# Squares by products, table rows for the sampled blocks, casts with two possible engines, and weights spread wider in a block-sparse attention and feed-forward kernel

## The chip, the cores and the metric

The kernel runs on one core of a Trainium2 chip. The time is what one execution takes on the device, in microseconds (us); several executions give a median. A profile shows one further execution, instruction by instruction. The engines are named as the profile names them: PE (matrix products), PEld (its weight loads), DVE (vector engine), ACT (scalar engine), POOL (GpSimd) and SP, whose queue starts nearly all transfers.

## The reference, cut to what matters

Four batches, eight heads, 768 positions of 64 numbers each. A query block of 32 positions sees its neighbours, the first and last block and three sampled blocks; the first and last query blocks see everything. The attention output is the input of a feed-forward layer with a maximum over three products.

```python
scores = scale * np.matmul(q, k.transpose(0, 1, 3, 2))
mask = np.abs(blk_i - blk_j) <= window
mask = mask | (blk_i == 0) | (blk_j == 0) | (blk_i == n_blocks - 1) | (blk_j == n_blocks - 1)
for qb in range(n_blocks):
    for kb in sampled_blocks[qb]:
        mask[qb * block:(qb + 1) * block, kb * block:(kb + 1) * block] = True
attn = softmax(np.where(mask, scores, -1000000000.0))
x = heads_joined(np.matmul(attn, v))                      # 3072 x 512
h = np.maximum(np.maximum(x @ w1, x @ w2), x @ w3)        # 3072 x 768
out = h @ w_out                                           # 3072 x 512
```

## The kernel before, in words

Every float32 operand is scaled by a power of two, got from the sum of its squares, and split in a high and a low float16 part; a product is three float16 products (high-high, high-low, low-high). So the first batch can't begin before the squares of its keys (`prep_k`, `kv_scale`) and queries (`prep_q`) are summed: ACT squares the tiles with a running sum (L498, L581), PE adds over the partitions with a matrix of ones (`total`, L354), DVE makes the scale (`scale_of`, L341 to L346). Then PE transposes the tiles (L528 keys, L597 queries), ACT writes the high part (L536, L601), DVE the low one (L539, L603). Values need no transposition (`prep_v`: L553 high, L557 low) and go to a scratch table in DRAM, from which POOL's indirect transfers fetch sampled rows (L651).

The work is 48 units, 12 per batch: one global unit "G" (the first and the last query blocks) and 11 sparse units of two query blocks. A sparse unit collects its keys: a window copy (L645, DVE) and six copies of sampled blocks (L638), whose addresses are read into registers of the copying engine (`value_load`, L329). Scores are L722 (L765 for G), the row maximum L700 (L697), the exponential L731 (L775), the probabilities' high and low parts L679 (ACT) and L680 (POOL), and a transposing transfer brings them to L746 (L787), the product with the values. For units below `TURNED` the transposition is done on PE (L672) with L674 (ACT) and L675 (DVE). `finish_unit` divides and transposes the result into `xg`, the feed-forward input; four units make one of its 12 blocks, which are called FFN0 to FFN11 here. A block is 216 products of 256 columns (L840) and 36 products of 512 columns (L864).

The weights arrive as float32 words of which the kernel needs some bits: a transfer (L390, L393) into staging tiles, a cast on POOL (L397), a shift and merge on DVE (L401), squares by 12 bfloat16 products of the tile with itself on PE (L419, the diagonal summed on DVE, L421), and the split (L434 ACT, L442 DVE).

The order on all engines comes from a planner: every piece of work is added with an engine, an assumed duration, what it reads and writes, and a priority; `order` walks through assumed time and gives each free engine the ready piece of lowest priority. The engines then run their lists in that order, each piece waiting for what it needs. Where the planner sees a gap on PE, `gaps` gives it filler: products of the identity matrix (L933), one per 0.11 us of the gap, into a feed-forward bank; nothing reads them.

Of the kernel before, what the change touches and what calls it, by code (L numbers as in the profile page):

```python
# [31 lines left out]
PV, TURNED, POOL_LOW = 0.2, 4, ()  # L32
TP, HOLD, WPRI, WSL = 0.45, 3.0, 3.0, 0.35
# [10 lines left out]
class Plan:  # L44
# [4 lines left out]
    SEM, DEPTH, START = 0.15, 6.0, 2.0  # L49
# [4 lines left out]
    def add(self, eng, us, emit, r=(), w=(), pri=0.0, land=None, mode=None, move=0.0, take=None, pair=False, drop=None, free=(), port=0, fresh=None):  # L54
        i = len(self.ops)
        deps = set()
# [4 lines left out]
        for key in w:  # L61
            deps.update(self.readers.get(key, ()))
            if key in self.wrote:
                deps.add(self.wrote[key])
            self.wrote[key], self.readers[key] = i, []
        for key in free:
            deps.update(self.readers.get(key, ()))
# [6 lines left out]
        self.ops.append(Op(eng=eng, us=us, emit=emit, deps=deps, pri=pri, land=land, mode=mode, move=move, take=take, pair=pair, drop=drop, port=port, fresh=fresh))  # L74

    def order(self, hold, switch):
# [7 lines left out]
        for i, op in enumerate(ops):  # L84
            cands.setdefault(op.eng, set())
            free.setdefault(op.eng, 0.0)
            if not left[i]:
                cands[op.eng].add(i)
# [12 lines left out]
        while len(out) < n:  # L101
            t, eng = min((max(free[e], min(map(at, c))), e) for e, c in cands.items() if c)
            now = [i for i in cands[eng] if at(i) <= t]
# [9 lines left out]
            cands[eng].remove(i)  # L113
# [30 lines left out]
            for s in succ[i]:  # L144
                same = ops[s].eng == eng and op.land is None
                ready[s] = max(ready[s], done + (0.0 if same else self.SEM))
                left[s] -= 1
                if not left[s]:
                    cands[ops[s].eng].add(s)
# [3 lines left out]
    def gaps(self):  # L153
# [13 lines left out]
def tile_block_sparse_attention_maxout_ffn(ctx, tc, q, k, v, sampled, w1, w2, w3, w_out, out):  # L167
# [90 lines left out]
    def sampled_rows():  # L258
# [5 lines left out]
        vi, oi1, oi2, row_in = (sbuf([N, NB], I32, x) for x in ("vi", "oi1", "oi2", "row_in"))  # L264
        zero = pts[NPT - 1][0:4, : H * VW // 2]

        def slot(dst, t, of):
            return lambda: Y.dma_start(
                out=dst[(3 + t) * HB : (4 + t) * HB],
                in_=bass.AP(s32.tensor, s32[0, of].offset, [[0, HB], [2 * NR, NB], [1, 1]]).rearrange("p n o -> p (n o)"),  # L270
            )

        def base():

            L.iota(vi, pattern=[[HB, NB]], base=-HB, channel_multiplier=1)
            L.iota(row_in, pattern=[[0, NB]], base=0, channel_multiplier=1)
            L.iota(rows_of, pattern=[[1, NB]], base=0, channel_multiplier=0)
            for x in (oi1, oi2):
                L.iota(x, pattern=[[0, NB]], base=-1, channel_multiplier=0)
# [3 lines left out]
        def shift():  # L283
            V.tensor_scalar(out=vi, in0=vi, scalar1=4, scalar2=None, op0=ALU.arith_shift_right)
# [6 lines left out]
        for t in range(NR):  # L291
            plan.add("SP", 0.45, slot(vi, t, t), r=["svi"], w=[("sv", t)], land=2.0, pri=-4)
        plan.add("SP", 0.45, slot(oi1, 1, 0), r=["svi"], w=[("so", 0)], land=2.0, pri=-4)
        plan.add("SP", 0.45, slot(oi1, 2, 0), r=["svi"], w=[("so", 1)], land=2.0, pri=-4)
        plan.add("SP", 0.45, slot(oi2, 2, 1), r=["svi"], w=[("so", 2)], land=2.0, pri=-4)
# [61 lines left out]


# [8 lines left out]
    w_stage = [(xg[i].rearrange("p g t x -> p (g t x)").bitcast(F32), XK(i)) for i in range(1, 3)]  # L367
    w_stage += [(stage[i], SK(i)) for i in range(6)]

    def stage_of(t):  # L370

        return w_stage[t] if t < 2 else w_stage[2 + (t - 2) % 7] if (t - 2) % 7 < 6 else w_stage[1]

    def decode_w(g, pri):
# [5 lines left out]
        for k in range(3):  # L380
# [19 lines left out]
            ), r=stk + ["yzero"], w=[yk], pri=pri)  # L400
# [10 lines left out]
        ss, tr = w_ss[c], {}  # L411
        mb = m.bitcast(BF16).rearrange("p k (x w) -> p k x w", w=2)[:, :, :, 1]

        def gram():

            for k in range(3):
                for x in range(4):
                    y = mb[:, k, x * P : (x + 1) * P]
                    T.matmul(out=bank(tr)[:, :P], lhsT=y, rhs=y, start=k == x == 0, stop=k == 2 and x == 3)  # L419
        plan.add("PE", 0.8, gram, r=mk, pri=pri, mode="t", take=tr)  # L420
        plan.add("DVE", 0.3, lambda: V.scalar_tensor_tensor(  # L421
            out=junk[:, :P], in0=bank(tr)[:, :P], scalar=1.0, in1=ident, op0=ALU.mult, op1=ALU.mult, accum_out=ss[:, 1:2]),
            r=["ident"], w=[("wss", c)], pri=pri, drop=tr)
# [4 lines left out]
    def split_w(g, parts, sc, keys, pri):  # L428
        m3, hi, lo, mk = parts
        for k in range(3):  # L430
# [4 lines left out]
                     r=mkk + keys, w=[("w", g, k, 0)], pri=pri)  # L435
# [10 lines left out]
    def prep_weights():  # L446
# [5 lines left out]
        for g in range(NF):  # L452
            split_w(g, decode_w(g, WPRI + WSL * g), [w_s[:, g : g + 1]], [("ws", g)], WPRI + WSL * g)
# [41 lines left out]
    def kv_scale(sts, sm, nm_, b, pri, more=None):  # L495

        for t in range(3):
            plan.add("ACT", 1.25, lambda t=t: A.activation(  # L498
                out=junk, in_=stage[sts[t]], func=AF.Square, accum_out=sm[:, t : t + 1]),
# [470 lines left out]
```

## Time and profile before

| | |
|---|---|
| median of 3 executions | 692.21 us (690.77 to 692.47) |
| profiled execution | 686.15 us, its span 684.3 us |
| mean granted PE clock in it | 0.978 |
| busy | PE 642.1, DVE 389.5, ACT 385.1, POOL 315.9 us |
| filler products (L933) | 671, 86.7 us of PE's busy time |
| products of FFN0 begin | 94.62 us |
| products of FFN1 begin | 183.32 us |

Read busy time by stage: the share over the whole span mixes a beginning, in which PE has too little to do, with some 500 us in which it is full. PE's busy time contains the filler, which is not work.

### The profile page before, as it was taken

Reading aid. Unit: us, or ns where it says so; the run is one execution under the profiler, and the core shown is the slowest. Engines: PE = TensorE matmul, PEld = TensorE weight load, DVE = VectorE, ACT = ScalarE, POOL = GpSimd, SP = SyncE. Lnnn points to the kernel's source line nnn. Section 1 sums busy time; section 2 is a strip of 40 time slices with the busy share of each in tenths; the row PEclk is TensorE's granted clock in tenths of the full one; section 3 lists DMA queues with packets and bytes.
Section 4 is the critical chain, followed back from the end, with each engine's and each line's share of the span. In section 5 each row is a group of like instructions: output and inputs, shape, how many; then the busy total and the mean of one; then the engine's idle time right before and its main releaser. Section 6 shows DMA issues by size and latency. Waiting matters only on the chain.

```text
span 684.3 us, 26761 instructions
## 1 busy us (share of the span) xinstructions
PE 642.1 (94%) x11319; PEld 495.5 (72%) x11319; DVE 389.5 (57%) x1050; ACT 385.1 (56%) x806; POOL 315.9 (46%) x414
## 2 busy tenths in 40 slices
PE   9799999998999998999999879999997999899997
PEld 7677778856887686687875666886774785678684
DVE  0289889966756775657457754364577664121110
ACT  1465766775738855864387764673786665112121
POOL 1324367723637575536167573373557576011110
PEclk9899999999999999999999999999999899899999
DMA  6589799976896999999849998886679689900000
GB/s 124 156 258 265 209 255 231 203 176 178 172 191 94 194 193 201 202 156 239 178 91 168 172 205 181 191 218 170 121 130 212 133 160 173 93 12 22 16 17 31
DMA packets 197051, 109.37 MB, mean 160 GB/s; under 512 B 161074, under 2 KB 182595, under 8 KB 196931
## 3 DMA queue, kind: packets, MB, share of 16 engines
q1 hardware_dynamic: 187074, 72.51, 55.9%
q0 software_dynamic: 9856, 35.15, 20.6%
q8 instruction: 88, 1.44, 1.0%
q14 instruction: 33, 0.26, 0.2%
HBM read 68.72 MB, written 12.70 MB: 119 GB/s over the span
## 4 chain that ended last, share of the span: by engine, by line
PE 79%; DVE 7%; issue 6%; DMA 5%; SPq 2%; ACT 1%; POOL 0%; DVEq 0%; ACTq 0%
PE f_ps L840 40%; PE f_ps L864 13%; PE av_ps L746 6%; PE f_ps L933 5%; PE s_ps L722 5%; DMA stage<-in_v_dram 2%; PE s_ps L765 2%; PE tp_ps L597 2%; DMA pts<-phl 2%; PE tp_ps L813 2%; PE av_ps L787 1%; DVE kt L401 1%; DVE w_hl L442 1%; PE tp_ps L528 1%; PE tp_ps L354 1%
## 5 line engine op out<-in xcount | busy, mean ns | idle before, releaser
L840 PE MATMUL f_ps<-xg,w_hl 128*128 128x256 f16 x2592 | 306.2, 277 | 3.0 <-issue 2.3
L840 PEld LDWEIGHTS <-w_hl 128*128 128x128 f16 x2592 | 252.5, 99 | 45.8 <-issue 11.4
L680 POOL TENSOR_TENSOR phl<-pr,phl 128x512 f16<-128x512 f32 (+1 forms) x106 | 120.2, 1139 | 74.1 <-ACT phl L679 35.5
L847 DVE SCALAR_TENSOR_TENSOR hf<-f_ps,hf 128x256 f32<-128x256 f32 x144 | 60.8, 422 | 115.2 <-PE f_ps L840 104.1
L851 POOL TENSOR_TENSOR ht<-hf,ht 128x256 f16<-128x256 f32 x72 | 51.3, 713 | 135.5 <-ACT ht L850 135.2
L651 POOL DMA_INDIRECT vg<-vscr,rows_of x88 | 83.5, 949 | 60.6 <-PE av_ps L746 43.8
L731 ACT ACTIVATE pr<-s_ps,nm,qsm 128x256 f32<-128x256 f32 x176 | 92.0, 562 | 21.8 <-DVE nm L703 20.4
L864 PE MATMUL f_ps<-wo_hl,ht 128*128 128x512 f16 x432 | 99.0, 380 | 2.5 <-issue 2.5
L933 PE MATMUL f_ps<-ident 128*128 128x256 f16 x671 | 86.7, 281 | 3.1 <-issue 1.6
L933 PEld LDWEIGHTS <-ident 128*128 128x128 f16 x671 | 66.0, 102 | 15.5 <-issue 5.2
L864 PEld LDWEIGHTS <-ht 128*128 128x128 f16 x432 | 40.6, 98 | 49.2 <-issue 5.5
L700 DVE TENSOR_REDUCE nm<-s_ps 128x2 f32<-128x512 f32 x88 | 60.2, 684 | 22.5 <-PE s_ps L722 21.7
L850 ACT CAST ht<-hf 128x256 f16<-128x256 f32 x72 | 29.0, 403 | 72.1 <-DVE hf L847 71.9
L679 ACT CAST phl<-pr 128x512 f16<-128x512 f32 (+1 forms) x106 | 62.6, 593 | 1.8
L746 PE MATMUL av_ps<-vg,pts 128*32 128x65 f16 (+1 forms) x4224 | 48.1, 195 | 10.5 <-issue 10.0
L746 PEld LDWEIGHTS <-pts 128*32 128x32 f16 x4224 | 39.5, 94 | 24.4 <-issue 22.0
L722 PE MATMUL s_ps<-kg,qt 64*32 64x256 f16 x2112 | 44.0, 275 | 11.4 <-issue 11.1
L638 POOL COPY kg<-kt 128x256 f16 x88 | 36.4, 435 | 33.5 <-PE s_ps L722 30.3
L638 ACT COPY kg<-kt 128x256 f16 x104 | 37.7, 403 | 19.3 <-PE s_ps L722 15.0
L844 ACT ACTIVATE hf<-f_ps 128x256 f32<-128x256 f32 x72 | 27.5, 382 | 37.1 <-PE f_ps L840 36.6
L870 ACT ACTIVATE ob<-f_ps,vsm 128x512 f32<-128x512 f32 x24 | 16.5, 686 | 44.2 <-PE f_ps L864 44.2
L722 PEld LDWEIGHTS <-qt 64*32 64x32 f16 x2112 | 23.3, 91 | 21.2 <-issue 18.2
(143 smaller groups left out, 668.8 us busy)
## 6 DMA issues: line engine op xcount, KB each, us to landing
stage<-in_moe_w_dram SPq DMA_DIRECT2D x14, 511.0 KB, 4.6
vscr<-vhl SPq DMA_DIRECT2D x12, 520.0 KB, 5.3
stage<-in_k_dram SPq DMA_DIRECT2D x24, 256.0 KB, 5.4
stage<-in_v_dram SPq DMA_DIRECT2D x12, 512.0 KB
qn<-in_q_dram SPq DMA_DIRECT2D x20, 256.0 KB, 5.5
out_dram<-ob SPq DMA_DIRECT2D x20, 256.0 KB, 2.4
stage<-in_moe_w_out_dram SPq DMA_DIRECT2D x5, 511.8 KB
vg<-vscr SPq DMA_DIRECT2D x16, 130.0 KB, 6.3
```

Of the source, the lines that this page charges most:

```text
L638: (A.copy if by == 2 else eng.tensor_copy)(out=dst, in_=src)
L651: plan.add("POOL", 1.02, lambda c=c: L.indirect_dma_start(out=vgj[: 6 * HB, c].rearrange("p e h x -> p (e h x)"), out_offset=None, in_=vsc ...
L679: plan.add("ACT", 0.05 + 0.565 * n / 512, lambda: A.copy(out=hl[:, :n], in_=prt[:, :n]), r=PRK(it), w=[hk], pri=pri)
L680: plan.add("POOL", 1.2 * n / 512, lambda: L.tensor_tensor(out=hl[:, n : 2 * n], in0=prt[:, :n], in1=hl[:, :n], op=ALU.subtract), r=PRK(it) ...
L700: plan.add("DVE", 0.7, lambda: V.tensor_reduce(out=n[:, 0:2], in_=both()[:, :, :256], axis=AX.X, op=ALU.max), w=[ks, (ks, 0), (ks, 1)], pr ...
L722: T.matmul(out=s_ps[r * BS : (r + 1) * BS, hd * 512 : hd * 512 + 256], lhsT=q_t[hp, tq, 2 * i + u, q0 + c * BS : q0 + (c + 1) * BS], rhs=k ...
L731: plan.add("ACT", 0.56, lambda hd=hd: A.activation(out=prt[:, hd * 256 : hd * 256 + 256], in_=s_of(job)[:, hd * 512 : hd * 512 + 256], fun ...
L746: T.matmul(out=av_ps[r * BS : (r + 1) * BS, 2 * i + hd, :w], lhsT=pv[:, tp, hd, e, r * BS : (r + 1) * BS], rhs=vgj[:, c, e, h, (D + 2) * t ...
L840: T.matmul(out=pf, lhsT=w_hl[f][:, j, g, wp], rhs=x[:, g, xp, :], start=g == 0 and n == 0, stop=g == G - 1 and n == 2)
L847: plan.add("DVE", 0.42, lambda h=h, pf=pf: V.scalar_tensor_tensor(out=h, in0=pf, scalar=2.0 ** -14, in1=h, op0=ALU.mult, op1=ALU.max), r=[ ...
L864: T.matmul(out=f2_ps, lhsT=hts[:, f, hp, t * P : (t + 1) * P], rhs=wo_hl[f // 3][:, f % 3, wp], start=f == 0 and n == 0, stop=f == NF - 1 ...
L933: T.matmul(out=f_ps[fb][:, :256], lhsT=x[:, :P], rhs=x, start=True, stop=True)
```

## The change

- The sums of squares of the first batch's keys and values and of its first queries are made on PE: `gram` multiplies each 128 columns of the tile's upper halfwords (bfloat16) with themselves, DVE sums the diagonal. ACT does it still for later batches.
- The six transfers that bring the sampled block numbers to partitions move whole table rows (139 to 143 words) instead of 24 single words each; the tiles they land in are wider, and every sixth word is used.
- The weights' cast (L397) may go to POOL or to ACT: the planner takes the one that would end first. The other alternatives that the diff lists stand behind `if 0`.
- For units below 8 the sampled copies are on DVE, POOL and ACT, one slot each, instead of ACT, POOL and ACT. Register loads follow: 8 at the beginning on DVE, 14 each on POOL and ACT, instead of 8 on POOL and 22 on ACT.
- The weights' priorities start at 2.0 and rise by 0.8 from one group to the next, instead of 3.0 and 0.35. The first values' priority goes from 0.2 to -1, `TURNED` from 4 to 2. The units run in the order G, 10, 8, 9, 0 to 7; the next batch's values and keys are prepared after the unit in place 6 instead of 4 (first batch).
- Filler is only put where the bank's earlier readers are already ordered, and the first filler is 3 us shorter.

Three places show what moves. On ACT at the start, `junk` is the target of the squares, `kt` and `qt` the keys and queries, `ksm`, `qsm` and `vsm` the columns with sums and scales. Before, from the last register load on:

```order
L329 TENSOR_LOAD samp
L329 ISA x2
L581 ACTIVATE junk,qsm_99<-qn 128x1024
L498 ACTIVATE junk,ksm_103<-stage_78 128x1024
L498 ACTIVATE junk,ksm_103<-stage_79 128x1024
L498 ACTIVATE junk,ksm_103<-stage_80 128x1024
L498 ACTIVATE junk,vsm_105<-stage_81 128x1024
L498 ACTIVATE junk,vsm_105<-stage_82 128x1024
L536 ACTIVATE kt_89<-s_ps_141,ksm_103 128x8x64
L601 ACTIVATE qt_97<-s_ps_141,qsm_99 128x4x128
L536 ACTIVATE kt_89<-tp_ps,ksm_103 128x8x64
```

And now:

```order
L351 TENSOR_LOAD samp
L351 ISA x2
L574 ACTIVATE kt_89<-s_ps_141,ksm_103 128x8x64 x2
L647 ACTIVATE qt_97<-tp_ps,qsm_99 128x4x128
L647 ACTIVATE qt_97<-s_ps_141,qsm_99 128x4x128
L574 ACTIVATE kt_89<-s_ps_141,ksm_103 128x8x64
L574 ACTIVATE kt_89<-tp_ps,ksm_103 128x8x64
L440 CAST ob_134<-xg_128 128x512
```

The seven squares are gone from ACT; its first work is the keys' high part, and two of the weights' casts come in.

On SP's queue at the start (`vi` and `oi` are the sampled numbers, `stage_81` to `stage_83` the values), before:

```order
L297 DMA vscr_136<-pts_122 4x520
L268 DMA vi<-in_sampled_blocks_dram 16x24x1 x3
L268 DMA oi_147<-in_sampled_blocks_dram 16x24x1 x2
L268 DMA oi_148<-in_sampled_blocks_dram 16x24x1
L489 DMA stage_81<-in_v_dram 128x8x128
L489 DMA stage_82<-in_v_dram 128x8x128
L489 DMA stage_83<-in_v_dram 128x8x128
L390 DMA xg_128<-in_moe_w_dram 128x4x511
```

And now:

```order
L319 DMA vscr_136<-pts_122 4x520
L523 DMA stage_81<-in_v_dram 128x8x128
L523 DMA stage_82<-in_v_dram 128x8x128
L290 DMA vi<-in_sampled_blocks_dram 16x143
L290 DMA vi<-in_sampled_blocks_dram 16x141
L290 DMA vi<-in_sampled_blocks_dram 16x139
L290 DMA oi_147<-in_sampled_blocks_dram 16x143 x2
L290 DMA oi_148<-in_sampled_blocks_dram 16x141
L523 DMA stage_83<-in_v_dram 128x8x128
L430 DMA xg_128<-in_moe_w_dram 128x4x511
```

Two of the three transfers of values pass the sampled numbers.

On ACT where FFN1 begins (`hf_130` is the first result of its products, `kt_90` the next batch's keys, `pr` and `phl` probabilities), before:

```order
L536 ACTIVATE kt_90<-tp_ps,ksm_104 128x8x64
L638 ISA
L638 COPY kg_92<-kt_90 128x256
L731 ACTIVATE pr_113<-s_ps_140,nm_108,qsm_101 128x256
L817 CAST xg_128<-tp_ps 128x4x64
L731 ACTIVATE pr_113<-s_ps_140,nm_108,qsm_101 128x256
L679 CAST phl_115<-pr_113 128x512
L731 ACTIVATE pr_114<-s_ps_141,nm_109,qsm_101 128x256
L817 CAST xg_129<-tp_ps 128x4x64
L731 ACTIVATE pr_114<-s_ps_141,nm_109,qsm_101 128x256
L679 CAST phl_116<-pr_114 128x512
L844 ACTIVATE hf_130<-f_ps_143 128x256
```

And now:

```order
L926 ACTIVATE ob_134<-f_ps_143,vsm_105 128x512
L533 ACTIVATE junk,vsm_106<-stage_79 128x1024
L926 ACTIVATE ob_135<-f_ps_144,vsm_105 128x512
L871 CAST xg_128<-tp_ps 128x4x64
L784 ACTIVATE pr_112<-s_ps_140,nm_108,qsm_101 128x256
L727 CAST phl_115<-pr_112 128x512
L784 ACTIVATE pr_113<-s_ps_141,nm_109,qsm_101 128x256
L533 ACTIVATE junk,vsm_106<-stage_80 128x1024
L784 ACTIVATE pr_113<-s_ps_141,nm_109,qsm_101 128x256
L898 ACTIVATE hf_130<-f_ps_143 128x256
L727 CAST phl_116<-pr_113 128x512
```

FFN1's first result now stands right behind the results of FFN0 (`ob`), ahead of the next batch's keys; before, the last of those keys stood ahead of it.

The diff, cut to its core:

```diff
-PV, TURNED, POOL_LOW = 0.2, 4, ()
-TP, HOLD, WPRI, WSL = 0.45, 3.0, 3.0, 0.35
+PV, TURNED, POOL_LOW = -1, 2, ()
+TP, HOLD, WPRI, WSL = 0.45, 3.0, 2.0, 0.8
...
+            best = {}
+            for i in set().union(*cands.values()):
+                if ops[i].alts:
+                    best[i] = min((max(free[a[0]], at(i)) + a[1], n) for n, a in enumerate(ops[i].alts))[1]
...
-                if nxt is not None and self.ops[nxt].fresh is not None:
-                    got[i] = (at[i] - (self.START if end is None else end), self.ops[nxt].fresh)
+                if nxt is not None and self.ops[nxt].fresh is not None and all(at[d] < at[i] for d in self.ops[nxt].seen):
+                    got[i] = (at[i] - (self.START + self.COLD if end is None else end), self.ops[nxt].fresh)
...
+            n = 2 * (NR * NB - of) - 1
             return lambda: Y.dma_start(
-                out=dst[(3 + t) * HB : (4 + t) * HB],
-                in_=bass.AP(s32.tensor, s32[0, of].offset, [[0, HB], [2 * NR, NB], [1, 1]]).rearrange("p n o -> p (n o)"),
+                out=dst[(3 + t) * HB : (4 + t) * HB, :n],
+                in_=bass.AP(s32.tensor, s32[0, of].offset, [[0, HB], [1, n]]),
             )
...
+    def gram(tiles, sm, r, w, pri):
+        job = {}
+        def mul():
+            xs = [x.bitcast(BF16).rearrange("p (x w) -> p x w", w=2)[:, c * P : (c + 1) * P, 1]
+                  for x in tiles for c in range(x.shape[1] // P)]
+            for n, y in enumerate(xs):
+                T.matmul(out=bank(job)[:, :P], lhsT=y, rhs=y, start=n == 0, stop=n == len(xs) - 1)
+        plan.add("PE", 0.06 * sum(x.shape[1] for x in tiles) / P, mul, r=r, pri=pri, mode="t", take=job)
+        plan.add("DVE", 0.3, lambda: V.scalar_tensor_tensor(
+            out=junk[:, :P], in0=bank(job)[:, :P], scalar=1.0, in1=ident, op0=ALU.mult, op1=ALU.mult, accum_out=sm),
+            r=["ident"], w=[w], pri=pri, drop=job)
...
-            ), r=stk + ["yzero"], w=[yk], pri=pri)
+            ), r=stk + ["yzero"], w=[yk], pri=pri, alts=[("ACT", 0.62, lambda st=st, y=y: A.copy(
...
+        if b:
+            for t in range(3):
+                plan.add("ACT", 1.25, lambda t=t: A.activation(
...
+        else:
+            for t in range(3):
+                gram([stage[sts[t]]], sm[:, t : t + 1], SK(sts[t]), (nm_, "ss", b, t), pri)
...
-                by = (2,1,2)[t] if pri < 8 else t
+                by = (0,1,2)[t] if pri < 8 else t
...
-    order = ["G", NU - 1] + list(range(NU - 1))
+    GROUPS = (2,0,1)
+    order = [m for g in GROUPS for m in (('G',10,8,9) if g == 2 else range(4 * g, 4 * g + 4))]
...
-        if x == (4 if U < 12 else 3) and b + 1 < B:
+        if x == max(gx, 6 if U < 12 else 6) and b + 1 < B:
             prep_v(b + 1, U + 3, [("unit", U)])
-        if x == (4 if U < 12 else 3) and b + 1 < B:
+        if x == (6 if U < 12 else 4) and b + 1 < B:
             prep_k(b + 1, U + 2, [("unit", U)])
```

More of the change, by code (lines that the diff above doesn't have):

```diff
@@ L83, in order, with offer @@
         dma, lock, banks = 0.0, 0.0, [0.0] * 5
-        for i, op in enumerate(ops):
-            cands.setdefault(op.eng, set())
-            free.setdefault(op.eng, 0.0)
+        for eng in ("PE", "DVE", "ACT", "POOL", "SP"):
+            cands[eng], free[eng] = set(), 0.0
+        def offer(i):
+            for eng in [a[0] for a in ops[i].alts] or [ops[i].eng]:
+                cands[eng].add(i)
+        for i in range(n):
             if not left[i]:
-                cands[op.eng].add(i)
+                offer(i)
         def choice(i):
@@ L410, in decode_w @@
             hi, lo = (wo_hl[g - NF][:, :, t] for t in range(2))
[L411 to L423, printed above, removed]
+        ss = w_ss[c]
+        gram([m[:, k] for k in range(3)], ss[:, 1:2], mk, ("wss", c), pri)
         sq, job = total([ss[:, 1:2]], [("wss", c)], pri)
@@ L799, in finish_unit @@
         x = un_no[0] % 2
+        pri -= 0
         un_no[0] += 1
```

167 lines of the change are left out of this document (99 added, 68 removed).

## The prediction

> **What bounds the kernel now.** The page first: is PE short of time or short of work?
>
> ```profile
> span 684.3 us, 26761 instructions
> PE 642.1 (94%) x11319; PEld 495.5 (72%) x11319; DVE 389.5 (57%) x1050; ACT 385.1 (56%) x806; POOL 315.9 (46%) x414
> L933 PE MATMUL f_ps<-ident 128*128 128x256 f16 x671 | 86.7, 281 | 3.1 <-issue 1.6
> ```
>
> PE is busy for 642.1 us, but 86.7 of them are filler (L933), so 684.3 = 555.4 of work + 86.7 of filler + 42.2 in which PE stands. Only the last two can shrink. Where they lie is told by the busy time by stage (the columns: PE, PEld, DVE, ACT, POOL, granted clock, share of the transfers, GB/s):
>
> ```profile
> 0.00:184.00 184.00, 168.59 (x2786) 135.23 (x2787) 128.08 (x326) 113.58 (x225) 81.77 (x126) 0.97 0.85 201
> 43.00:95.00 52.00, 48.59 (x974) 37.65 (x971) 45.91 (x111) 35.88 (x76) 21.63 (x31) 1.00 0.96 257
> 95.00:152.00 57.00, 56.33 (x964) 45.03 (x962) 49.79 (x128) 40.64 (x86) 34.23 (x38) 1.00 1.00 205
> 184.00:600.00 416.00, 393.31 (x7909) 298.88 (x7907) 247.91 (x692) 255.63 (x546) 224.12 (x274) 0.98 0.89 170
> ```
>
> and by the same view of L933 alone (PE, PEld, then as above):
>
> ```profile
> 0.00:184.00 184.00, 85.52 (x663) 65.23 (x663) 0.97 0.85 201
> 152.00:184.00 32.00, 18.49 (x148) 13.98 (x148) 0.95 0.72 169
> ```
>
> By 184 us PE has had 85.5 us of filler and stood for 15.4 (184 less 168.6), and has done 83.1 us of work. Behind that there is 1 us of filler, and PE stands for 22.7 of 416 us. So a change can gain before FFN1 begins, at 183.32; what follows is PE's own work. In that beginning DVE is the other full engine: 95.7 of 109 us (88%) from 43 to 152. The first 43 us are a chain, in the timeline:
>
> ```profile
> 1.49 20.32 PE L933 MATMUL f_ps<-ident 128*128 128x256 f16 x164 [1.49 <-DVE ident L250]
> 12.15 2.89 SPq L268 DMA_DIRECT2D oi<-in_sampled_blocks_dram  x3
> 15.22 1.06 ACT L581 ACTIVATE junk<-qn 128x1024 bf16<-128x1024 f32 x1 [12.98 <-issue]
> 22.41 0.16 DVE L341 TENSOR_SCALAR ksm<-tp_ps 128x1 int32<-128x1 int32 x1 [19.88 <-PE tp_ps L354]
> 25.29 1.06 ACT L498 ACTIVATE junk<-stage 128x1024 bf16<-128x1024 f32 x1 [5.38 <-DMA stage<-in_v_dram]
> 28.82 1.11 PE L597 MATMUL s_ps<-ident,qn 128*128 128x128 f32 x4 [4.40 <-ACT kt L536]
> 42.71 1.16 PE L765 MATMUL s_ps<-kt,qt 64*64 64x384 f16 x12
> 94.62 1.58 PE L840 MATMUL f_ps<-xg,w_hl 128*128 128x256 f16 x13
> 183.32 1.91 PE L840 MATMUL f_ps<-xg,w_hl 128*128 128x256 f16 x16
> ```
>
> ACT does nothing that counts until 15.22: for 12.98 us it reads 22 registers, 0.59 each. Then it squares, and the keys' scale starts at 22.41. Then ACT stands at the squares of the values, which came late behind the sampled numbers' single words; the keys' first high part stands behind them in its list, and PE behind that for 4.40. The first scores start at 42.71.
>
> **The change, part by part.** The changed program's order gives counts; prices come from rows of this trace.
>
> ```profile
> L419 PE MATMUL tp_ps<-kt 128*128 128x128 bf16 x72 | 5.1, 219 | 0.0
> L421 DVE SCALAR_TENSOR_TENSOR junk<-tp_ps,ident 128x128 bf16<-128x128 f32 x6 | 1.7, 280 | 0.0
> L675 DVE TENSOR_TENSOR pts<-tp_ps,pts 128x384 f16<-128x384 f32 (+1 forms) x7 | 4.2, 605 | 0.0
> L638 DVE COPY kg<-kt 128x256 f16 x72 | 27.8, 406 | 8.1 <-issue 8.1
> L539 DVE SCALAR_TENSOR_TENSOR kt<-tp_ps,ksm,kt 128x512 f16<-128x512 f32 x21 | 15.6, 745 | 9.1 <-ACT kt L536 9.1
> L700 DVE TENSOR_REDUCE nm<-s_ps 128x2 f32<-128x512 f32 x88 | 60.2, 684 | 22.5 <-PE s_ps L722 21.7
> 617.52 23.58 PE f_ps L840 x216
> 23.83 0.60 PE L528 MATMUL tp_ps<-ident,stage 128*128 128x128 f32 x4
> 556.07 0.38 PE L813 MATMUL tp_ps<-ident,xr 128*128 128x128 f32 x2
> 556.38 0.85 PE L722 MATMUL s_ps<-kg,qt 64*32 64x256 f16 x48
> 562.50 0.98 PE L746 MATMUL av_ps<-vg,pts 128*32 128x65 f16 x96
> ```
>
> *PE's work.* Squares: 56 more products at 71 ns (5.1 us for 72), +4.0. `TURNED`: 10 instead of 14 calls of four transpositions, taken at the 0.60 of L528's four, -2.4. Together +1.6.
>
> *Filler.* The order has 561 instead of 671. A product of 256 columns takes 109 ns (23.58 us for 216), so 110 fewer are 12.0 us. This is the main term, and it is a saving only if PE doesn't stand in their place. Bounds: 0, if each one left out leaves its gap open (the new condition in `gaps` drops filler without closing the gap); 14.2, at the mean that filler had, 129 ns (86.7 us for 671, with the slow start in it). I take 12.0, for the reason in the stages that follow.
>
> *The start.* ACT now reads 14 registers, done by about 10.5 (2.24 + 14 x 0.59), and has no squares. The keys have landed by about 12, where the transfers' share drops from 1.20 to 0.28:
>
> ```profile
> 11.00:12.00 1.00, 1.00 (x11) 0.90 (x10) 0.00 (x0) 0.00 (x0) 0.00 (x0) 1.00 1.20 192
> 12.00:13.00 1.00, 1.00 (x11) 0.90 (x10) 0.00 (x0) 0.00 (x0) 0.00 (x0) 1.00 0.28 28
> ```
>
> But the squares on PE stand in line behind filler: 16, then 28 ahead of each tile of keys. At the pace of the first 164 these 100 take 12.4 us, to 13.9; with four groups of eight squares (0.57 each) and the steps between, PE is through the keys near 17. The diagonal on DVE (0.28 and a read), five more fillers and the sum put the scale at about 20 instead of 22.41. So the squares alone bring 2 to 3 us, not the 7 that ACT was late. Behind them the values' squares are off ACT's list, and two of the three value transfers pass the sampled numbers, so the 4.40 goes. I expect scores at 33 to 35 instead of 42.71. This is no term of its own: it is in the filler's count.
>
> *Weights and units until FFN1.* FFN0 has 467 fillers ahead of it instead of 428: not earlier than before, perhaps some us later. But between its second product and FFN1 stand 14 instead of 151, since FFN1 no longer stands behind the next batch's keys. At FFN1's first product the sums are: filler 553 instead of 663, -12.0; 1.5 sparse units fewer (0.85 + 0.98 + 0.38 each), -3.3; six key transpositions later, -3.6; +1.6 from above. FFN1 starts 17.3 earlier, at 166, with 5.3 + 1.6 = 6.9 us more work behind it.
>
> *DVE until then.* New: 16 sampled copies at 406 ns, 6.5; seven diagonals at 0.36, 2.5; some seven more register loads in its stream at ACT's 0.59, 4.1. Gone: four low parts at 605 ns, 2.4; six of keys at 745 ns, 4.5; 1.5 units, each with two maxima at 684 ns and an estimated three times 1 us for the rest, 6.5. About even: DVE's 127 us of work would fall between 18 and 166, 86% of that time, where 88% was reached from 43 to 152. It fits with little room, and if it doesn't, each us of DVE is one of PE.
>
> *ACT, POOL, SP.* ACT loses seven squares and 16 copies, and takes 13 of POOL's 24 casts. From 43 to 152 ACT was busy for 70% and POOL for 51% (76.5 and 55.9 of 109), so I cost these at nothing: DVE, the engine that the casts feed, hides them; without that cover a cast is 0.9 us in the weights' line. Transposing transfers rise from 106 to 110, on transfers that have a share of 0.89 behind 184.
>
> *Sum.* 684.3 + 1.6 - 12.0 = 673.9, with PE standing for 42 us as before: less the 4.40, and as much again for four new waits on transfers in PE's list. The profiled execution was 1.85 us longer than its span (686.15), and the median of the runs shown is 6.06 above that, so I move the median by the same 10.4: 681.8.
>
> **What the clock does when PE stands.** Behind the 4.40 the clock fell, and the fillers there took twice their time:
>
> ```profile
> 28.00:34.00 6.00, 5.18 (x26) 4.07 (x27) 2.67 (x4) 3.07 (x7) 1.53 (x2) 0.55 0.47 151
> 29.73 2.56 PE L933 MATMUL f_ps<-ident 128*128 128x256 f16 x11
> ```
>
> About half of the 5.18 us is lost that way, 2.3 us. By these rows an open gap of that size costs 4.4 + 2.3, and leaving filler out is dearer than the filler. The Trainium skill ("TensorE: Matmul & The Clock Gate", "What's actually happening") says that the clock is halved after an idle window of about 3.4 us and is full again after a busy one of that length; the trace agrees here. Were three of the dropped fillers' gaps that long, the sum by it would be some 5 us higher.
>
> **The rivals.**
>
> *The gaps stay open (about the same time).* The 12 us are filler that the planner didn't write, not time that went. For it: the condition in `gaps` does just that; DVE has 21 us of room in 148; the planner assumes 0.22 us for a copy that takes 0.406. Against it: from 43 to 95 the old order came out nearly as planned, with PE busy for 48.59 of 52. The price is the 12 us back, 685.9 in the span less what other waits give up, or 692 in the median with one gap's slow clock left out on both sides. It decides if FFN1 begins at 176 or later.
>
> *The end loses its cover (slower).* Behind the last turned unit stood long, undisturbed products:
>
> ```profile
> 580.42 4.18 issue
> 604.29 0.22 PE tp_ps L813 x2
> 672.45 7.78 PE f_ps L864 x36
> ```
>
> These are 76 us, from 604.5 to 680.2. In the new order there are 240 short and 72 long ones (0.216 each): 26.2 + 15.5 = 42. To be no slower, attention must end by 638 (684.3 less the 4.1 behind PE, less 42). From FFN1 at 166 PE's work until then is 437 us (555.4 + 1.6 - 77.8 - 42), with the 24 that it stood or filled 627: 11 us of room. Four more waits like the 4.18 us above, late transposing transfers that no feed-forward product covers, decide against it: 673.9 + 16.7 = 690.6, in the median 698.5. Against it: the trace had 35 sparse units in 421 us at a share of 0.89; now 36.5 have 461, so the transfers are less crowded.
>
> *Fewer waits (faster still).* For that same reason the 22.7 us of standing behind 184 could fall to 8: 659 in the span, 667 in the median. Against it: these waits come from a list written by assumed times, and a new list has new ones.
>
> **How the numbers follow.** The forecast, 681.8, has a chance of 0.55; open gaps at 692, 0.14; the end's cover at 698.5, 0.12; fewer waits at 667, 0.19. The forecast's own range is 674 to 689 (the upper half of the filler's bounds, and some us of standing either way). To leave out no more than 2 in 10 the range is 668 to 694: a little of the third rival, and the first whole. A difference of 0.3% (2 us) is about what a measurement of this kernel can tell from none. Faster by more than that: 0.53 of the forecast, the third rival, 0.05 of the first: 0.77. Within it: 0.02 and 0.07: 0.09. Slower: 0.02 of the first and the second: 0.14.
>
> **What would show it.** In the changed profile: filler (L991) at 561 products and near 73 us; the keys' scale at about 20; the first scores (L818) at 33 to 35; FFN1's first product near 166; DVE busy for 85 to 90% until then; PE standing for about 42 us in all. I am wrong in the start if L818 comes after 40; in the main term if FFN1 begins after 176 with little filler and long waits of PE; at the end if the last unit is turned (L867) after 638.

## The result

| | before | after |
|---|---|---|
| median of 4 executions | 692.34 us | 674.24 us (666.68 to 680.57) |
| profiled execution | 686.15 us | 669.58 us |
| ratio to the kernel before | 1 | 0.9653 (0.9608 to 0.9699) |
| ratio, with more executions | 1 | 0.9661 (0.9590 to 0.9733) |

By the ratio the change makes the kernel 3.4% faster; 681.8 us (1.5%) was forecast. The executions of the changed kernel lie in two groups, around 668 and 680 us, of which the ratios take the lower one alone, and by the medians over all executions the gain is 2.6%.

The page after; L991 is the filler:

```profile
span 667.8 us, 26558 instructions
PE 626.4 (94%) x11249; PEld 482.8 (72%) x11249; DVE 382.4 (57%) x1076; ACT 379.8 (57%) x789; POOL 314.1 (47%) x405
L991 PE MATMUL f_ps<-ident 128*128 128x256 f16 x561 | 71.6, 277 | 1.5 <-DVE ident L268 1.5
```

So 667.8 = 554.8 of work + 71.6 of filler + 41.4 of standing, where 557.0 + 74.7 + 42.2 was forecast. In the timeline, the marks in the order in which the prediction named them: the keys' scale, the first scores, the first product of FFN0 and of FFN1, the last turned unit.

```profile
18.18 0.16 DVE L363 TENSOR_SCALAR ksm<-s_ps 128x1 int32<-128x1 int32 x1 [0.81 <-PE s_ps L376]
34.79 1.52 PE L818 MATMUL s_ps<-kt,qt 64*64 64x384 f16 x24
100.63 2.78 PE L894 MATMUL f_ps<-xg,w_hl 128*128 128x256 f16 x24
164.88 1.47 PE L894 MATMUL f_ps<-xg,w_hl 128*128 128x256 f16 x12
621.07 0.38 PE L867 MATMUL tp_ps<-ident,xr 128*128 128x128 f32 x2
```

FFN1 begins 18.4 us earlier than at 183.32 (17.3 forecast). Behind it the kernel before needed 501.0 us to the end of the span, the changed one needs 502.9: 1.9 us more, where 6.9 was forecast. That is where most of the surplus lies, and the busy time by stage shows it (columns as before: PE, PEld, DVE, ACT, POOL, granted clock, share of the transfers, GB/s):

```profile
0.00:184.00 184.00, 165.31 (x2814) 135.09 (x2815) 128.43 (x350) 109.26 (x210) 82.62 (x118) 0.98 0.92 210
18.00:165.00 147.00, 131.11 (x2322) 105.73 (x2322) 112.67 (x296) 93.17 (x181) 69.96 (x93) 0.98 0.93 215
184.00:600.00 416.00, 398.53 (x7766) 299.31 (x7765) 240.33 (x691) 256.52 (x547) 221.24 (x274) 1.00 0.84 167
600.00:668.00 68.00, 62.54 (x674) 48.45 (x671) 13.66 (x36) 14.04 (x33) 10.22 (x15) 1.00 0.18 37
```

From 184 to 600 PE stands for 17.5 us instead of 22.7, and its granted clock is 1.00 instead of 0.98; until 184 it stands for 18.7 (15.4 before), behind 600 for 5.3 (4.1). DVE is busy for 77% of the time from 18 us to FFN1, not for 85 to 90%.

What got shorter is seen at the scores of the sparse units, over the whole run (idle time of PE before them in the last column; before, then after):

```profile
L722 PE MATMUL s_ps<-kg,qt 64*32 64x256 f16 x2112 | 44.0, 275 | 11.4 <-issue 11.1 <-DVE kg L645 0.2
```

```profile
L775 PE MATMUL s_ps<-kg,qt 64*32 64x256 f16 x2112 | 45.7, 272 | 5.8 <-issue 3.1 <-ACT xg L871 1.2 <-ACT wo_hl L466 0.7
```

The 11.1 us were four waits, the longest 4.4; the longest now is 1.4. What ended them the profile doesn't show ("issue").

### The profile page after: what moved, and what is told of

The parts are those of the page before. It is cut to its first block, busy times and chain, and to the rows that moved or that the text cites. A ratio compares the mean times of both kernels' runs of the same rounds, so it can differ in the third digit from the quotient of the medians.

```text
span 667.8 us, 26558 instructions
## 1 busy us (share of the span) xinstructions
PE 626.4 (94%) x11249; PEld 482.8 (72%) x11249; DVE 382.4 (57%) x1076; ACT 379.8 (57%) x789; POOL 314.1 (47%) x405
## 2 busy tenths in 40 slices
DMA packets 199065, 110.45 MB, mean 165 GB/s; under 512 B 162993, under 2 KB 184610, under 8 KB 198946
## 4 chain that ended last, share of the span: by engine, by line
PE 83%; issue 4%; DMA 4%; DVE 4%; ACT 3%; another core or an unknown queue 0%; SPq 0%; DVEq 0%; POOL 0%; ACTq 0%; POOLq 0%
PE f_ps L894 42%; PE f_ps L920 13%; PE av_ps L799 6%; PE s_ps L775 6%; PE f_ps L991 5%; DMA pts<-phl 2%; PE s_ps L818 2%; PE tp_ps L867 2%; PE tp_ps L643 2%; PE av_ps L840 1%; PE tp_ps L566 1%; DMA vscr<-vhl 1%; PE tp_ps L376 1%; PE tp_ps L388 1%; DVE nm L749 1%
## 5 line engine op out<-in xcount | busy, mean ns | idle before, releaser
L728 POOL TENSOR_TENSOR phl<-pr,phl 128x512 f16<-128x512 f32 (+1 forms) x110 | 126.8, 1155 | 110.2 <-ACT phl L727 74.0
L991 PE MATMUL f_ps<-ident 128*128 128x256 f16 x561 | 71.6, 277 | 1.5 <-DVE ident L268 1.5
L727 ACT CAST phl<-pr 128x512 f16<-128x512 f32 (+1 forms) x110 | 65.2, 594 | 2.2 <-DMA pts<-phl 0.3
L991 PEld LDWEIGHTS <-ident 128*128 128x128 f16 x561 | 53.8, 100 | 10.4 <-issue 2.3
L799 PEld LDWEIGHTS <-pts 128*32 128x32 f16 x4224 | 39.5, 95 | 22.7 <-issue 19.6
L775 PE MATMUL s_ps<-kg,qt 64*32 64x256 f16 x2112 | 45.7, 272 | 5.8 <-issue 3.1
L685 ACT COPY kg<-kt 128x256 f16 x88 | 31.6, 402 | 26.1 <-PE s_ps L775 21.2
L754 DVE TENSOR_SCALAR nm<-nm,qsm 128x1 f32<-128x1 f32 x192 | 32.5, 207 | 2.3
```

The source lines that it names most:

```text
L685: (A.copy if by == 2 else eng.tensor_copy)(out=dst, in_=src)
L727: plan.add("ACT", 0.05 + 0.565 * n / 512, lambda: A.copy(out=hl[:, :n], in_=prt[:, :n]), r=PRK(it), w=[hk], pri=pri, alts=[("DVE", 0.6 * n ...
L728: plan.add("POOL", 1.2 * n / 512, lambda: L.tensor_tensor(out=hl[:, n : 2 * n], in0=prt[:, :n], in1=hl[:, :n], op=ALU.subtract), r=PRK(it) ...
L775: T.matmul(out=s_ps[r * BS : (r + 1) * BS, hd * 512 : hd * 512 + 256], lhsT=q_t[hp, tq, 2 * i + u, q0 + c * BS : q0 + (c + 1) * BS], rhs=k ...
L799: T.matmul(out=av_ps[r * BS : (r + 1) * BS, 2 * i + hd, :w], lhsT=pv[:, tp, hd, e, r * BS : (r + 1) * BS], rhs=vgj[:, c, e, h, (D + 2) * t ...
L991: T.matmul(out=f_ps[fb][:, :256], lhsT=x[:, :P], rhs=x, start=True, stop=True)
```

## The experiments

The kernel before had medians of 684 to 693 us in different groups of runs, so only the ratios to it, taken within a group, are compared; a mark or a span is of one profiled execution. All 18 at a glance (filler in the order; FFN1's first product and the span in the profile, us):

| kernel | filler | FFN1 | span | ratio |
|---|---|---|---|---|
| before | 671 | 183.3 | 684.3 | 1 |
| changed (a_again) | 561 | 164.4 | 668.8 | 0.9661 (0.9590 to 0.9733) |
| changed, words again (a_words) | 561 | 175.1 | 680.7 | 0.9843 (0.9782 to 0.9903) |
| before, rows (b_rows) | 671 | 179.5 | 676.0 | 0.9947 (0.9898 to 0.9996) |
| before, preparation and spread (b_prepspread) | 608 | 171.1 | 686.2 | 0.9986 (0.9936 to 1.0036) |
| before, rows, preparation, spread (b_rowsprepspread) | 608 | 158.7 | 664.3 | 0.9755 (0.9666 to 0.9844) |
| before, filler rule (b_fillrule) | 644 | 192.4 | 691.3 | 1.0015 (0.9974 to 1.0056) |
| before, no filler (b_nofill) | 0 | 187.8 | 688.0 | 0.9982 (0.9944 to 1.0020) |
| changed, no filler (a_nofill) | 0 | 161.4 | 665.9 | 0.9605 (0.9551 to 0.9659) |
| the same (a_nofill_again) | 0 | 152.5 | 652.8 | 0.9641 (0.9572 to 0.9709) |
| three parts, no filler (b_three_nofill) | 0 | 160.1 | 663.1 | 0.9768 (0.9702 to 0.9833) |
| changed, old preparation (a_oldprep) | 699 | 194.6 | 689.6 | 1.0011 (0.9976 to 1.0047) |
| changed, old spread (a_nospread) | 680 | 180.1 | 694.0 | 1.0023 (0.9981 to 1.0066) |
| changed, squares on ACT (a_actsq) | 646 | 173.3 | 671.7 | 0.9811 (0.9730 to 0.9893) |
| changed, old copies (a_copies) | 634 | 174.3 | 688.7 | 1.0005 (0.9967 to 1.0043) |
| changed, casts on POOL (a_poolcast) | 675 | 165.3 | 685.3 | 1.0118 (1.0050 to 1.0186) |
| changed, nudged (a_nudge) | 619 | 173.5 | 684.4 | 0.9948 (0.9906 to 0.9991) |
| changed, nudged otherwise (an_12) | 558 | 162.9 | 666.9 | 0.9785 (0.9697 to 0.9874) |
| before, nudged (b_nudge) | 698 | 194.4 | 698.8 | 1.0156 (1.0106 to 1.0206) |

**The changed kernel again.**

> The changed kernel unchanged, for more executions. If the gain is the filler and standing that left the time before FFN1, plus the half-clock stretches that the kernel before has behind its long late waits, the ratio to the kernel before stays at 0.960 to 0.970. If the first result was drawn from a few lucky executions, it comes back to my forecast of 0.985.

0.9661: the gain stands, and the forecast of 0.985 is outside the interval.

**Is filler a price?** The kernel before with the new rule for filler, then both kernels without filler:

```diff
-                if nxt is not None and self.ops[nxt].fresh is not None:
-                    got[i] = (at[i] - (self.START if end is None else end), self.ops[nxt].fresh)
+                if nxt is not None and self.ops[nxt].fresh is not None and all(at[d] < at[i] for d in self.ops[nxt].seen):
+                    got[i] = (at[i] - (self.START + self.COLD if end is None else end), self.ops[nxt].fresh)
```

> The kernel before with only the new rule for filler: its work order is the same, 27 of 671 fillers are left out, all of them at the start. If the filler is only an indicator of time in which PE waits for others: 0 us, within 0.3%. If a filler left out is 0.11 us saved by itself: 3 us faster. If the start needs them to have full speed at its first real products: 1 to 3 us slower.

```diff
-        for _ in range(int(us * 1.0 / 0.11)):
+        for _ in range(0):
```

> The kernel before without any filler; the order of the work is the same, and all that is computed is computed. If filler costs PE's time where the work could have gone on: faster, by up to the part of 86.7 us that was in the way. If it fills gaps that are there anyway (the theory on which the forecast rests): the span doesn't fall; the gaps become standing of about 80 us, and with gaps of over 4 us the granted clock falls in the first 184 us, so 3 to 12 us slower.

> The changed kernel without any filler, the order of its work the same. If the change gained by writing less filler, the two kernels without filler are within 1% of each other. If it gained because the work comes earlier, the changed order still leads by 12 to 24 us, and it is itself 2 to 10 us slower than with filler, by the lower clock before FFN1.

The rule alone does nothing that can be measured. Nor does leaving out all of it in the kernel before (page, a stage by its busy time, and FFN1's first product):

```profile
span 688.0 us, 25420 instructions
PE 595.7 (87%) x10648; PEld 445.8 (65%) x10648; DVE 382.8 (56%) x1050; ACT 384.6 (56%) x806; POOL 313.3 (46%) x414
```

```profile
43.00:95.00 52.00, 38.62 (x758) 26.48 (x757) 41.07 (x104) 32.16 (x71) 18.26 (x25) 0.68 0.89 238
```

```profile
187.75 1.49 PE L840 MATMUL f_ps<-xg,w_hl 128*128 128x256 f16 x6
```

Now the granted clock falls to 0.68 from 43 to 95 us, and the same work takes 595.7 us instead of 555.4. But the span is only 3.7 us longer, and the ratio is 0.998. PE stands for 92.3 us where it stood or filled for 128.9: most of the 40 us that the slow products cost lie in time that was filler. So 109 ns is not what leaving out a filler saves; the count is a gauge of how long the list makes PE wait. Whether the slow clock costs nothing, or about what the filler had cost, this run doesn't separate. The changed kernel without filler keeps its lead, 0.9605 against 0.9982, so the lead is not a saving of filler; nor is it slower than with filler, as was expected (2 to 10 us):

```profile
span 665.9 us, 25437 instructions
PE 593.1 (89%) x10688; PEld 445.4 (67%) x10688; DVE 385.4 (58%) x1076; ACT 380.4 (57%) x789; POOL 313.2 (47%) x405
```

```profile
161.43 1.47 PE L894 MATMUL f_ps<-xg,w_hl 128*128 128x256 f16 x12
```

Whether filler brings the upper group of times was asked with more executions:

> The changed kernel without filler once more, for more executions. If the filler brings the slower executions of the changed kernel, all times lie within 664 to 669. If the four times so far were lucky, half of them lie at 677 to 684.

They lay between 653.6 and 663.6 us beside 676.7 to 693.3 of the kernel before on that chip, without two clear groups. Neither expectation fits, so the cause of the groups stays open. Of all kernels run, this one has the lowest ratios, below the kernel before by 3.6 to 4.0%; its lead on the changed kernel lies inside the intervals.

**The table rows, with the order unchanged.** Words instead of rows in the changed kernel, and rows in the kernel before. Neither edit moves an instruction in the lists.

```diff
-                out=dst[(3 + t) * HB : (4 + t) * HB, :n],
-                in_=bass.AP(s32.tensor, s32[0, of].offset, [[0, HB], [1, n]]),
+                out=dst[(3 + t) * HB : (4 + t) * HB].rearrange("p (n w) -> p n w", w=2 * NR)[:, :, 0],
+                in_=bass.AP(s32.tensor, s32[0, of].offset, [[0, HB], [2 * NR, NB], [1, 1]]).rearrange("p n o -> p (n o)"),
```

> The changed kernel with the sampled block numbers brought as single words again, 16 x 24 of them per transfer; the order of the work on every engine is the same. If the table rows only take work off the transfer queue that nobody waits for: within 0.3% of the changed kernel. If the first copies and value transfers behind them wait: 2 to 5 us slower, with L818 and the keys' scale later by as much.

This is the largest effect that one edit had with the same list, and more than the 2 to 5 us expected: 1.8% between the ratios, and in the profiled executions 12.9 us of span and 10.2 us at FFN1. The busy time from 14 to 22 us tells where it begins (last two columns: share of the transfers, GB/s). The kernel before, the same with rows, the changed kernel, and the changed kernel with words:

```profile
14.00:22.00 8.00, 8.00 (x76) 7.21 (x74) 0.00 (x0) 4.60 (x8) 1.98 (x9) 1.00 0.14 10
```

```profile
14.00:22.00 8.00, 8.00 (x77) 7.19 (x74) 0.00 (x0) 6.80 (x12) 4.71 (x20) 1.00 0.93 251
```

```profile
14.00:22.00 8.00, 7.65 (x77) 6.80 (x75) 2.02 (x14) 1.46 (x3) 2.67 (x12) 1.00 0.77 222
```

```profile
14.00:22.00 8.00, 7.46 (x75) 6.62 (x73) 2.16 (x14) 1.65 (x3) 1.15 (x5) 1.00 0.35 69
```

With single words the transfers nearly stop, 10 GB/s against 251 with rows in the kernel before. In the changed kernel two value transfers pass the words, so that the stop lies from 16 to 24 us, and the lines for 14 to 22 us show 69 GB/s against 222. The packets of the whole run are 199065 with rows and 201273 with words: 2208 more, which are 6 x 16 x 24 words less 6 x 16 rows. In the changed kernel with words it is the first weights, next on SP's queue, that come late (timeline, ACT and PE, the wait in brackets):

```profile
30.29 0.76 ACT L440 CAST ob<-xg 128x512 f16<-128x512 bf16 x1 [3.70 <-DMA xg<-in_moe_w_dram]
30.92 0.68 ACT L574 ACTIVATE kt<-s_ps,ksm 128x512 f16<-128x512 f32 x1
32.69 0.88 PE L566 MATMUL s_ps<-ident,stage 128*128 128x128 f32 x4 [2.38 <-DVE junk L390]
35.65 3.79 PE L991 MATMUL f_ps<-ident 128*128 128x256 f16 x17
39.37 1.71 PE L818 MATMUL s_ps<-kt,qt 64*64 64x384 f16 x24
175.13 1.14 PE L894 MATMUL f_ps<-xg,w_hl 128*128 128x256 f16 x9
```

The third and fourth of these in the changed kernel:

```profile
30.72 0.66 PE L566 MATMUL s_ps<-ident,stage 128*128 128x128 f32 x4 [0.22 <-DVE junk L390]
32.85 2.02 PE L991 MATMUL f_ps<-ident 128*128 128x256 f16 x17
```

A cast waits at the head of ACT's list, the keys' high part stands behind it, DVE's low part and its sums of diagonals behind that, and PE behind those: it turns the next keys at 32.69 instead of 30.72. Then the granted clock is 0.50 (34 to 38 us), the 17 fillers ahead of the scores take 3.79 us instead of 2.02, and the first scores come 4.6 us later. How these grow to 10.2 us at FFN1 is not shown.

> The kernel before with table rows for the sampled blocks alone; its order is otherwise the same, 671 fillers. If the transfers' idle time at the start is a term by itself, the values land some 8 us earlier, PE's 4.40 us of standing at 24 us and the slow clock behind it go, the first scores come at 34 to 37 instead of 42.71, and it is 5 to 12 us faster. If the list behind the start was written for later data and only waits elsewhere: within 0.3%.

In the kernel before, the same edit takes the first scores from 42.71 to 37.99 and FFN1 from 183.32 to 179.47:

```profile
37.99 1.16 PE L768 MATMUL s_ps<-kt,qt 64*64 64x384 f16 x12
...
179.47 4.09 PE L843 MATMUL f_ps<-xg,w_hl 128*128 128x256 f16 x36
```

That gains 0.5%, some 3.6 us, less than the 5 to 12 expected: FFN1 still stands behind the next batch's keys.

**Preparation, spread, and both with the rows.**

```diff
-TP, HOLD, WPRI, WSL = 0.45, 3.0, 3.0, 0.35
+TP, HOLD, WPRI, WSL = 0.45, 3.0, 2.0, 0.8
-        if x == (4 if U < 12 else 3) and b + 1 < B:
+        if x == 6 and b + 1 < B:
             prep_v(b + 1, U + 3, [("unit", U)])
-        if x == (4 if U < 12 else 3) and b + 1 < B:
+        if x == (6 if U < 12 else 4) and b + 1 < B:
             prep_k(b + 1, U + 2, [("unit", U)])
```

> The kernel before with two numbers of the change alone: the weights' priorities (2.0, 0.8) and the next batch prepared after place 6 (4 for later keys). 608 fillers instead of 671. If these two carry the main term and the start (squares, table rows, copies, casts) adds only the 8 us of the first scores: 7 to 9 us faster than the kernel before. If the gain needs the parts together, since DVE and ACT have no room without the start: under 3 us. If the order decides alone: the whole gain, 17 us or more.

> Table rows, moved preparation and spread weights together in the kernel before: 608 fillers. If the three add up, 10 to 17 us faster than the kernel before, since the spread and the preparation gave under 1 us without the rows. If the new copies and casts are needed as well, under 5 us.

Rows alone 0.5%, preparation and spread 0.1%, the three together 2.45%. The interval of the three together overlaps that of the whole change. FFN1 then begins earlier than in the changed kernel:

```profile
158.69 1.03 PE L843 MATMUL f_ps<-xg,w_hl 128*128 128x256 f16 x8
```

The same two parts, taken back in the changed kernel one at a time (each by its old numbers, 4 and 3, and 3.0 and 0.35):

> The changed kernel with the next batch's values and keys prepared after the unit in place 4 again (3 in later batches). Its order has 699 fillers instead of 561 and two more sparse units ahead of FFN1. If the move of this preparation is what gained, it loses by the forecast's own price (109 ns for a filler) 15.0 us to the changed kernel, by the 137 ns that the fillers left out took 18.9, so about 682 to 685 beside 667 to 670, and FFN1 begins at about 184. If the order of the first batch is only luck, it is within 5 us.

> The changed kernel with the weights' priorities at 3.0 and 0.35 as before. Its order has 680 fillers instead of 561; FFN0 stands behind 421 instead of 467, FFN1 behind 613 instead of 553. If the weights' spread is needed beside the moved preparation: 13.0 us slower than the changed kernel by 109 ns, 16 by 137 ns. If the moved preparation carries the gain alone: within 4 us of the changed kernel, and the extra filler stands where PE waits anyway.

Each loses the whole gain, more than the count said (15.0 and 13.0 us; the ratios lose 3.5 and 3.6%, 24 and 25 us). With the old preparation FFN1 begins at 194.62, later than in the kernel before:

```profile
194.62 1.58 PE L894 MATMUL f_ps<-xg,w_hl 128*128 128x256 f16 x13
```

**The three parts against the whole, without filler.**

> The kernel before with table rows, moved preparation and spread weights, and without filler. If these three carry the change, it comes within 0.5% of the changed kernel without filler, whose ratio to the kernel before was 0.9605 and 0.9641. If squares on PE, copies, casts and the units' order are worth several us by themselves: 0.970 to 0.980.

0.9768, where the whole change had 0.9605 and 0.9641: the rest of the change, with its order, is worth some 1.3 to 1.6%. The interval is clear of that of the first of the two and just touches that of the second.

**The start's other parts, and the casts.** The squares go back to ACT (keys and values, then queries), the sampled copies and register loads to the engines that had them, and the casts to POOL alone.

```diff
-        if b:
+        if True:
...
-        if c:
+        if True:
```

> The changed kernel with the first batch's sums of squares on ACT as before, all else unchanged: 56 products of 71 ns less on PE (4.0 us), 85 fillers more (9.3 us at 109 ns). Net 5.3 us slower if the start's earlier scores are worth what the filler's count says. 4 us faster if the units that come earlier only wait for the weights, so that the squares on PE are a pure cost.

```diff
-                by = (0,1,2)[t] if pri < 8 else t
+                by = (2,1,2)[t] if pri < 8 else t
-        by = (0,1,2)[t] if 8 > 0 else t
+        by = (2,1,2)[t] if 8 > 4 else t
-        registers(t, by, many if by else many[:8], -9 + t / 10)
+        registers(t, by, many[:8] if t else many, -9 + t / 10)
```

> The changed kernel with the sampled copies and register loads on the engines that had them before (ACT, POOL, ACT; DVE none). 634 fillers instead of 561. By the count 9.3 us slower; if DVE has no room for its 16 copies, so that they cost what they save, within 2 us.

```diff
-            ), 0)] if 1 else ())
+            ), 0)] if 0 else ())
```

> The changed kernel with the weights' casts on POOL alone: 675 fillers instead of 561. By my forecast the casts cost nothing wherever they are, so within 3 us of the changed kernel (ratio to the kernel before 0.962 to 0.970). By the count of filler at 128 ns, 14.6 us slower than the changed kernel (0.985 to 0.990).

The squares move the start hardly at all. With them on ACT the keys' scale comes at 18.84 (18.18 with PE) and the first scores at 34.87 (34.79): with fewer registers to read ahead of them, ACT begins its squares at 10.32 instead of 15.22.

```profile
18.84 0.16 DVE L363 TENSOR_SCALAR ksm<-tp_ps 128x1 int32<-128x1 int32 x1 [10.27 <-PE tp_ps L376]
34.87 1.16 PE L818 MATMUL s_ps<-kt,qt 64*64 64x384 f16 x12
```

Still the kernel with squares on ACT loses 1.5% to the changed kernel, at intervals that just touch, and copies and casts lose 3.5 and 4.6%. That is two to three times what the counts had said (5.3, 9.3 and 14.6 us). The casts show that such a loss need not lie where the part lies: they are needed before FFN1, and FFN1 begins at 165.28 as in the changed kernel. What is lost is lost behind it. The filler there, by the busy time of L991 alone, with casts on POOL and in the changed kernel:

```profile
184.00:600.00 416.00, 12.05 (x93) 9.29 (x93) 0.98 0.87 163
```

```profile
184.00:600.00 416.00, 1.20 (x8) 0.78 (x8) 1.00 0.84 167
```

and all of it, with casts on POOL:

```profile
184.00:600.00 416.00, 388.63 (x7539) 298.44 (x7538) 238.58 (x671) 249.20 (x531) 210.51 (x264) 0.98 0.87 163
```

PE fills or stands for 39.4 us (27.4 and 12.05) where the changed kernel has 18.7 (17.5 and 1.2). The list behind FFN1 is another one.

**How much is the list itself?** One number of the planner that belongs to no part of the change, the assumed time of a semaphore, 0.16 (0.12 in an_12), and in the kernel before 0.16 too:

```diff
-    SEM, DEPTH, START, COLD = 0.15, 6.0, 2.0, 3.0
+    SEM, DEPTH, START, COLD = 0.16, 6.0, 2.0, 3.0
```

> The changed kernel with one number of the planner that belongs to no part of the change: the assumed time of a semaphore 0.16 instead of 0.15 us. It moves the whole order (619 fillers instead of 561). If such an order gains by its parts, it stays within 3 us of the changed kernel. If a list is worth what its count of filler says, 58 more at 128 ns make it 7.4 us slower, about 675 to 678 in the profile. If the whole gain was drawn by luck: 15 us or more slower.

> The kernel before with the same number at 0.16: 698 fillers instead of 671. By the count 3.5 us slower; by luck alone anything from 15 us faster to 10 slower; if the parts decide, within 3 us.

> The changed kernel with the assumed semaphore time at 0.12 us: another order with 558 fillers, 427 of them ahead of FFN0 and 554 ahead of FFN1. If the count of filler tells the time, within 3 us of the changed kernel (span 665 to 671). If the changed kernel's order is lucky beyond its count, 5 to 15 us slower, by more standing of PE.

The nudge costs the changed kernel about 3%, most of its gain, and the kernel before 1.6%. By the expectation on record this is the case of a gain drawn by luck. The other nudge, with a count like that of the changed kernel, has a ratio 1.2% higher, but the intervals overlap, and by the medians of all executions (0.975 and 0.974 of the kernel before) there is no difference. In the first nudged one, from 184 us on:

```profile
184.00:600.00 416.00, 394.53 (x7608) 299.49 (x7614) 243.02 (x691) 254.59 (x545) 216.21 (x270) 0.98 0.87 165
```

PE stands for 21.5 us instead of 17.5. So a rearranged list alone can move this kernel by 1.6 to 3%, and the losses of the parts taken back may hold that much of mere order. Priced by the count, from the changed kernel on (128 ns each, 4.0 us off for the squares), the seven rearranged kernels come out at 0.965 to 0.991; measured, each lies above that, by 0.5 to 2.5%. By the medians of all executions the same differences are -0.7 to 1.4%, so it is not shown that the changed kernel's list is better than its count.

## Why the prediction was right and wrong

*What bounds it* was right for the beginning: FFN1 moved by 18.4 us (17.3). "What follows is PE's own work" was not right: 5.0 us were gained behind FFN1, and the kernel with casts on POOL, with the same FFN1, lost its whole gain there.

*The step that failed is the last one of the sum*, "with PE standing for 42 us as before", together with the 6.9 us of moved work that I charged in full to the time behind FFN1. The span fell by 16.5 us, 6.1 more than forecast. By terms, the filler measured 15.1 us (86.7 less 71.6: 137 ns for each of the 110) instead of 12.0, the work -0.6 instead of +1.6, and the standing 41.4 instead of 42.2. By place, the 3.1 us more of filler lay before 184 us, and 3.3 us more of standing there took them up again. Behind it PE stood for 5.2 us less until 600 and 1.2 more after that, with the clock at 1.00 instead of 0.98, so that only 1.9 of the 6.9 us remained. Why this list waits less there stays open: under the nudged list, which has all parts of the change, PE stands for 21.5 us from 184 to 600 instead of 17.5.

The rest of the miss in the median (18.1 against 10.4) is how far each median stands above its profiled execution, 6.2 before and 4.7 now, which I had held constant. By the ratio the gain is 24 us; 16.6 of them stand between the two profiled executions, and for the others there is no trace.

*Fewer waits*, the rival at 667, was right in direction and about a third of its size: 5.2 of the 14.7 us. *The end loses its cover* fell: the last unit was turned at 621.07, and the end cost 1.2 us more. *The gaps stay open* fell too, as stated: FFN1 came before 176.

*The start came out for a reason that I had not given.* The scores came at 34.79, inside my 33 to 35. I put it down to the squares (2 to 3 us) and to values that pass the words in SP's queue. The squares measured 0.7 us at the keys' scale and nothing at the scores. With words put back the values still pass them, and the scores come at 39.37. I had quoted the row from 12 to 13 us, with a share of 0.28, and read it as "the keys have landed"; it was the beginning of some 8 us in which the transfers moved next to nothing. The table rows, which I gave no term, carry 4.6 us at the scores, 10.2 at FFN1 and 1.8% of the time: a term that the sum lacks. With the words put back the ratio is 0.9843, close to the 0.985 forecast, but with FFN1 at 175.13 and not at 166. A mark that is hit doesn't show that its reason is right.

*Casts, copies and spread at nothing or within room.* Taking any of them back loses the gain, but the nudges and the casts' profile show that much of this can be the list and not the part. How much of the 3.4% belongs to each stays open, apart from the rows, and these are worth 1.8% in the changed list and 0.5% in the old one. DVE had more room than I allowed, 77% busy instead of 86.

*Filler dearer to leave out than to keep* fell. I carried over what one open gap does to the clock, 2.3 us behind 4.4. Without any filler the slow clock is there, and the time is the same within 0.6%. Nor does "the trace agrees here" hold in full: in that gap of 4.40 us the clock fell after 2.2 us, at 26.6, and it was full at 33.4, 4.6 us after PE had work again. In the changed kernel with words it fell behind a wait of 2.38 us.

## What to carry over

Before an edit is costed, look for stretches in which the transfers have a queue and move nothing, and ask which row ends them. In a kernel whose lists come from a planner, an edit that leaves the lists as they are can be measured; one that rearranges them has to be set beside a few rearrangements that mean nothing; here two of three were worth 1.6 and 3%. Parts of such a change don't add up (0.5, 0.1, together 2.45%), so neither undoing one nor doing one alone tells what it is worth.

## What the runs showed of the hardware

Behind six transfers of 16 x 24 single words all transfers of the kernel before moved 10 GB/s for 8 us; with the same numbers as table rows, six times the bytes, they moved 251 GB/s. And without any filler the granted clock fell to 0.68 (43 to 95 us) and 0.64 (152 to 184 us), with 40 us more for the same products, and yet the time of the kernel before moved by no more than 0.6% (the interval of the ratio, 0.9944 to 1.0020).
